# Moving the row ends of one gradient to GpSimd and packing a shift-weight gradient in 32-column tiles

## The chip, the core and the metric

The kernel runs on one core of one Trainium2 chip. Its time is the device time of one execution in microseconds (us); of several executions the median is taken. The engines of the core each work through an instruction queue of their own, in order: TensorE (PE in the profile; its weight loads are PEld), VectorE (DVE), ScalarE (ACT), GpSimd (POOL), and SyncE (SP), which here only issues DMA transfers. The engines wait for each other by semaphores. Matmul results go to PSUM and have to be copied out by DVE or ACT before their PSUM buffer is free again.

## The reference, cut to what matters

The function is a sum of a skip connection, a state-space block with a shift convolution and a long convolution, and a bilinear feed-forward block; the kernel returns its value and nine gradients. With S = 2048 rows, D = 512 channels, F = 1376:

```
xn  = layernorm(x)                                  # x = A_q
ks  = sum_j  shift(k, j) * shift_k[:, j]            # j = 0..3, shift along S
kv  = ks * v
y   = causal long convolution of kv with ssm_k (by FFT), + kv * ssm_D
out = x + xn * y + ((xn Wg) * (xn Wu)) Wd           # out_0
```

From `grad_out` come out_1 (gradient of x), out_2 (k), out_3 (v), out_4 (shift_k, D x 4), out_5 (ssm_k, D x S), out_6 (ssm_D) and out_7 to out_9 (the three weights). Two of them matter here:

- out_1 = grad_out + layernorm backward of dxn. In the kernel each row end is `rstd * dxn + m1`, then `+ grad_out`.
- out_4[d, j] = sum over the sequence of dks[s + j, d] * k[s, d], where dks is the gradient of ks. The kernel takes it from TensorE as the diagonal of small Gram matrices: dks as weights against four shifted copies of k, all products of a group of channels with each other, of which only the diagonal is kept.

## The kernel before, in words

The sequence is laid out as 128 partitions times R = 16 rows. There are three stages. First the inputs are normalised and transformed while the feed-forward block runs chunk by chunk; second the spectral products and their inverse run beside the rest of the feed-forward block. Neither is touched. The third stage, from about 340 us to the end, is the one at hand.

Its backbone is `dw` (L803): for each of 11 blocks of F it transposes the hidden activations (L704, PSUM tile `pt`, copied to `nath` and `natd` by ACT), forms out_9 (L814, `pd`) and out_7 and out_8 (L831, `pu`; the copies are `od` and `og`). The blocks of hidden activations come back from DRAM with `load_hb` (L688). `dw` is a generator of 66 steps, and after each step the side generators of L973 are advanced, each from a first step on and then every so many steps:

- `seq(inv_y(), load_kh(), load_dk())` from step 0, every 3: the inverse transforms `pq` (L729) that give `yC` and, times v, `dks`; then the 2.3 MB load `khC` of k with its three shifted rows (L941 to L943); then two loads `gk` of 1 MB (L769).
- `dsk_gram()` from step 30, every 2: the Gram matrices of out_4. For each of four groups of 128 channels it takes a two-bank PSUM tile `pk` of the pool ps2, and 32 matmuls of 64 columns by 256 (L853): two halves of 64 channels, 16 rows each. DVE multiplies each half by the identity (`kd`, L858) and reduces it (L860).
- `inv_dk()` from step 41, every 3: eight groups of 16 matmuls `po` (L784) for out_5. The even ones are copied to `o5t` by DVE, the odd ones by ACT (L785).
- `ew()` from step 10, every 2: the elementwise ends, from the list `tail`. `final(r)` (L897) first issues the loads of x and of the feed-forward part `bb` for row r + 1 (L892, L894), then forms out_0 (L906 to L909) and dxn with its two row sums (L911 to L919) on DVE. `final2(r)` (L924) applies `rstd` and `m1` on ACT, `final3(r)` (L931) adds grad_out on DVE and stores out_1 from SP (L934). They are run one row late: final2(r - 1), final(r), final3(r - 1). After each two rows `bwd(b)` (L874) computes two rows of out_2: seven DVE operations on `dk` and `tk` and a store (L886).

The PSUM pool ps2 (`P2`) has three buffers, shared by `pt`, `pu`, `pq`, `pk` and `po`; ps1 (`P1`) has two, shared by `pd`, `ptd` and `pts`. A scheduler of the language orders the instructions of each engine from this program; within one engine they then run strictly in that order. So a PE instruction that needs a PSUM buffer waits for the copy that empties it, and that copy waits for everything ahead of it on ACT or DVE. The SBUF pool c2b holds two buffers each of `dxn`, `o1`, `o0`, `bb` and `dk`. `o5t` and `khC` share one buffer (tag o5k). SP's DMAs use eight completion semaphores in turn, so that a DMA is issued only once the eighth one before it has landed.

Of the kernel before, what the change touches and what calls it, by code (L numbers as in the profile page):

```python
# [8 lines left out]
BF = mybir.dt.bfloat16  # L9
F32 = mybir.dt.float32  # L10
I32 = mybir.dt.int32
ALU = mybir.AluOpType
ACTF = mybir.ActivationFunctionType
AX = mybir.AxisListType
# [4 lines left out]
D = 512  # L19
F = 1376  # L20
R = 16
P = 128
NC4 = 4
# [132 lines left out]
def kernel(  # L156
# [24 lines left out]
    nc = tc.nc  # L181
# [10 lines left out]
    o1_n = nat(out_1[0])  # L192
# [9 lines left out]
    def dve(o, i):  # L202
        nc.vector.tensor_copy(o, i)  # L203
# [13 lines left out]
    def P2(name, shape, dt=F32):  # L217
        return ps2.tile(shape, dt, name=name, tag="p2")

    def P1(name, shape, dt=F32):  # L220
        return ps1.tile(shape, dt, name=name, tag="p1")

    ident = const.tile([P, P], BF, name="ident")
# [7 lines left out]
    rstd = const.tile([P, R], F32, name="rstd")  # L231
# [313 lines left out]
    def seq(*its):  # L545
        for it in its:
            for _ in it:
                yield
# [128 lines left out]
    goC = c1.tile([P, R, D], BF, name="goC")  # L677
# [39 lines left out]
    dks = c2.tile([P, R + 3, D], BF, name="dks")  # L717
# [21 lines left out]
    def inv_y():  # L739
        gq = pend  # L740
        todo = [(sg, r0) for r0 in range(0, R, 4) for sg in (0, 1)][2:]
        for r4 in range(0, R, 4):
            gy = gq.pop(0)
            vk = [load_vk(r4), load_vk(r4 + 2)]
            for i in range(0, 4, 2):
                st1p(gy, i, yC[:, r4 + i:r4 + i + 2, :])
            if todo:
                gq.append(load_g1(*todo.pop(0)))
            yield
            gd = gq.pop(0)  # L750
            for i in range(0, 4, 2):
                r0 = r4 + i
                vb, kb = vk.pop(0)
                dd = c2b.tile([P, 2, D], BF, name="dd")
                st1p(gd, i, dd[:])
                nc.vector.tensor_tensor(dks[:, r0:r0 + 2, :], dd[:], vb[:], op=ALU.mult)
                nc.vector.tensor_tensor(kb[:], dd[:], kb[:], op=ALU.mult)
                nc.sync.dma_start(o3_n[:, r0:r0 + 2, :], kb[:])
                if r0 == 2:
                    nc.gpsimd.memset(dks[96:128, R:R + 3, :], 0.0)  # L760
                    nc.sync.dma_start(dks[0:112, R:R + 3, :], dks[1:113, 0:3, :])
                    nc.sync.dma_start(dks[112:127, R:R + 3, :], dks[113:128, 0:3, :])
            if todo:
                gq.append(load_g1(*todo.pop(0)))
            yield
# [8 lines left out]
    def inv_dk():  # L774
        o5t = c2.tile([P, NC4, P, R], BF, name="o5t", tag="o5k")
        o5 = out_5.rearrange("(c q) s -> c q s", q=P)
        steps = [(dh, rh) for dh in range(2) for rh in range(2)]
        for n, (dh, rh) in enumerate(steps):
            gk = gks.pop(0)
            for b in range(2):  # L780
                po = P2("po", [P, 8, P])
                for i in range(8):
                    for c in range(2):
                        nc.tensor.matmul(po[:, i, :], lhsT=gk[:, c, i, cs(b)], rhs=TB.IW[:, c, :], start=(c == 0), stop=(c == 1))  # L784
                (act if b else dve)(o5t[:, 2 * dh + b, :, 8 * rh:8 * rh + 8], po[:].rearrange("q r s -> q s r"))  # L785
                if rh == 1:
                    nc.sync.dma_start(o5[2 * dh + b], o5t[:, 2 * dh + b].rearrange("q s r -> q (s r)"))
                if b == 1 and n + 2 < len(steps):
                    gks.append(load_gk(*steps[n + 2]))
                yield  # L790
            if n == 2:
                yield from put_dD(o5t)
# [52 lines left out]
            yield  # L845

    def dsk_gram():
        for c in range(NC4):
            pk = P2("pk", [P, 2, D])
            for r in range(R):  # L850
                for h in range(2):
                    c0 = c * 128 + 64 * h
                    nc.tensor.matmul(pk[64 * h:64 * h + 64, h, 0:256], lhsT=dks[:, r, c0:c0 + 64],  # L853
                                     rhs=KH[0][:, r:r + 4, c0:c0 + 64], start=(r == 0), stop=(r == R - 1))
            kd = c2.tile([P, 4, 64], F32, name="kd")
            for h in range(2):
                hs = slice(64 * h, 64 * h + 64)
                nc.vector.tensor_tensor(kd[hs], pk[hs, h, 0:256].rearrange("q (j c) -> q j c", j=4),  # L858
                                        ident[hs, hs].unsqueeze(1).to_broadcast((64, 4, 64)), op=ALU.mult)
            nc.vector.tensor_reduce(dsk[:, c, :], kd[:], axis=AX.X, op=ALU.add)  # L860
            yield
        dskb = c2.tile([P, 4, NC4], BF, name="dskb")
        nc.vector.tensor_copy(dskb[:], dsk[:].rearrange("q c i -> q i c"))
        for _ in range(2):
            yield
        pt = P1("pts", [P, 4, P], BF)
        for j in range(4):
            nc.tensor.transpose(pt[:NC4, j, :], dskb[:, 3 - j, :], ident[:])
        dskt = c2.tile([NC4, P, 4], BF, name="dskt")
        dve(dskt[:], pt[:NC4].rearrange("c j q -> c q j"))  # L870
        nc.sync.dma_start(out_4.rearrange("(c p) j -> c p j", p=128), dskt[:])
        yield
# [24 lines left out]
    def final(r):  # L897
        if r + 1 < R:
            load_fin(r + 1)
        o, bb = FL.pop(r)  # L900
        tt = nc.vector.tensor_tensor
        xn = xnC[:, r, :]
        go = goC[:, r, :]
        y = yC[:, r, :]
        m = c2.tile([P, D], BF, name="mf")
        tt(m[:], xn, y, op=ALU.mult)  # L906
        tt(o[:], m[:], o[:], op=ALU.add)
        tt(o[:], o[:], bb[:, 0, :], op=ALU.add)
        nc.sync.dma_start(o0_n[:, r, :], o[:])  # L909
        e = c2.tile([P, D], BF, name="e")  # L910
        tt(e[:], go, y, op=ALU.mult)  # L911
        dxn = c2b.tile([P, D], F32, name="dxn")
        nc.vector.scalar_tensor_tensor(dxn[:], e[:], 1.0, bb[:, 1, :], op0=ALU.mult, op1=ALU.add,
                                       accum_out=s1[:, r:r + 1])
        nc.vector.scalar_tensor_tensor(e[:], dxn[:], 1.0, xn, op0=ALU.mult, op1=ALU.mult,
                                       accum_out=s2[:, r:r + 1])
        nc.vector.tensor_scalar(m2[:, r:r + 1], s2[:, r:r + 1], -1.0 / D, None, op0=ALU.mult)
        nc.vector.tensor_scalar(m1[:, r:r + 1], s1[:, r:r + 1], rstd[:, r:r + 1], -1.0 / D, op0=ALU.mult, op1=ALU.mult)
        nc.vector.scalar_tensor_tensor(dxn[:], xn, m2[:, r:r + 1], dxn[:], op0=ALU.mult, op1=ALU.add)  # L919
        DX[r] = dxn  # L920

    DX = {}

    def final2(r):  # L924
        o1 = c2b.tile([P, D], BF, name="o1")
        nc.scalar.activation(o1[:], DX.pop(r)[:], ACTF.Identity, bias=m1[:, r:r + 1], scale=rstd[:, r:r + 1])
        O1[r] = o1

    O1 = {}

    def final3(r):  # L931
        o1 = O1.pop(r)
        nc.vector.tensor_tensor(o1[:], o1[:], goC[:, r, :], op=ALU.add)
        nc.sync.dma_start(o1_n[:, r, :], o1[:])  # L934

    KH = []

    def load_kh():
        khC = c2.tile([P, R + 3, D], BF, name="khC", tag="o5k")
        nc.gpsimd.memset(khC[0:1, 0:3, :], 0.0)  # L940
        nc.sync.dma_start(khC[:, 3:3 + R, :], k_n)  # L941
        nc.sync.dma_start(khC[1:113, 0:3, :], k_n[0:112, R - 3:R, :])
        nc.sync.dma_start(khC[113:128, 0:3, :], k_n[112:127, R - 3:R, :])  # L943
        KH.append(khC)
        yield

    def every(gen, start, step):
        return [start, step, gen]

    tail = []  # L950
    for b in range(9):
        if b < 8:
            for r in (2 * b, 2 * b + 1):
                tail.append(lambda r=r: (r > 0 and final2(r - 1), final(r), r > 0 and final3(r - 1)))
        else:
            tail.append(lambda: final2(R - 1))
            tail.append(lambda: final3(R - 1))
        if b > 0:
            tail.append(lambda b=b: bwd(b - 1))

    def ew():
        load_fin(0)
        yield
        for f in tail:
            f()
            yield

    def load_dk():
        gks.append(load_gk(0, 0))
        gks.append(load_gk(0, 1))  # L970
        yield

    sides = [every(seq(inv_y(), load_kh(), load_dk()), 0, 3), every(dsk_gram(), 30, 2), every(inv_dk(), 41, 3), every(ew(), 10, 2)]  # L973
    for n, _ in enumerate(dw()):
        for sd in sides:
            if n >= sd[0]:
# [35 lines left out]
```

## Time and profile before

| | us |
|---|---|
| three executions | 529.89, 533.33, 533.99 |
| median | 533.33 |
| the profiled execution | 530.92 |
| its span (first to last instruction) | 528.9 |
| PE busy | 486.2 (92%) |
| DVE busy | 344.9 (65%) |
| ACT busy | 339.2 (64%) |
| POOL busy | 8.5 (2%) |
| third stage, 340 us to the end | 189 |
| PE busy in the third stage | 175.2 |
| DVE busy in the third stage | 119.7 |
| 16 DMA engines, share of the span by SP's queue | 80.3% |

The span is what the profile shows; the execution's own time has 2.0 us around it, and the median lies 2.4 us above that execution. In the profile a group or timeline line gives start, duration, engine, line of the kernel, operation, output and inputs, and in square brackets how long the engine had been idle and who ended it. "Lx" is line x of the kernel before.

### The profile page before, as it was taken

What the parts mean: (1) busy time and instruction counts of PE and PEld (TensorE: products, weight loads), DVE (VectorE), ACT (ScalarE), POOL (GpSimd) and SP (SyncE); (2) the same over time, 40 slices, a digit from 0 to 9 for tenths busy, and PEclk for the clock granted to TensorE, in tenths of its full rate; (3) what the DMA queues carried; (4) which work ended last, traced back from release to release, by engine and by line L of the source; (5) the groups of instructions that cost most, each with busy time, mean ns of one, the idle gap of its engine ahead of it and who ended that gap; (6) DMA issues with size and microseconds to landing.
All of it is one profiled execution on the core that took longest, in us unless ns stands there. A gap on an engine that the chain in (4) does not pass through costs nothing.

```text
span 528.9 us, 10804 instructions
## 1 busy us (share of the span) xinstructions
PE 486.2 (92%) x4409; PEld 322.6 (61%) x4409; DVE 344.9 (65%) x678; ACT 339.2 (64%) x377; POOL 8.5 (2%) x18
## 2 busy tenths in 40 slices
PE   2998999999799999997998999999999999959996
PEld 2876665456436546544535764467677777847885
DVE  5876979876385867837857760042787688899520
ACT  3586798768449859766949861286587444654451
POOL 3100000000000000000000000020000000000000
PEclk9999999999999999998999999999999999989999
DMA  9987988998947967956944459899999998888814
GB/s 284 344 297 290 318 262 315 319 307 311 298 154 260 254 213 257 273 192 217 264 161 147 158 186 405 304 330 325 372 336 311 351 313 268 277 253 252 264 50 133
DMA packets 106570, 140.53 MB, mean 266 GB/s; under 512 B 19001, under 2 KB 79517, under 8 KB 106010
## 3 DMA queue, kind: packets, MB, share of 16 engines
q1 hardware_dynamic: 105194, 139.07, 80.3%
q10 hardware_dynamic: 1328, 0.79, 0.5%
q8 instruction: 34, 0.56, 0.4%
q14 instruction: 14, 0.11, 0.1%
HBM read 72.89 MB, written 63.41 MB: 258 GB/s over the span
## 4 chain that ended last, share of the span: by engine, by line
PE 42%; DMA 22%; DVE 16%; ACT 11%; issue 5%; SPq 3%; DVEq 0%; ACTq 0%
PE px L473 13%; PE pgu L438 7%; PE pu L831 5%; DMA out_dram<-dk 5%; PE py L467 5%; DMA o<-in_A_q_dram 3%; PE pdh L444 3%; ACT SP L200 2%; DMA khC<-in_A_k_dram 2%; DMA out_dram<-o 2%; DMA FD<-fst 2%; PE pd L814 2%; PE pg L531 2%; ACT gu L200 2%; DMA v_b<-in_A_v_dram 2%
## 5 line engine op out<-in xcount | busy, mean ns | idle before, releaser
L831 PE MATMUL pu<-natd,xnC 128*128 128x256 bf16 (+1 forms) x704 | 80.7, 273 | 6.1 <-ACT nath L200 5.9
L473 PE MATMUL px<-WT,hd 128*128 128x512 bf16 (+1 forms) x352 | 81.4, 383 | 0.0
L831 PEld LDWEIGHTS <-xnC 128*128 128x128 bf16 x704 | 68.1, 99 | 15.0 <-issue 6.5
L438 PE MATMUL pgu<-xt,Wu 128*128 128x256 bf16 (+1 forms) x352 | 54.7, 279 | 6.6 <-DVE SP L504 4.1
L473 PEld LDWEIGHTS <-hd 128*128 128x128 bf16 (+1 forms) x352 | 33.8, 98 | 43.5 <-issue 5.2
L200 ACT CAST gu<-pgu 128x1024 bf16<-128x1024 f32 (+1 forms) x48 | 45.4, 946 | 17.3 <-PE pgu L438 16.3
L518 DVE TENSOR_TENSOR T<-SP 128x2048 bf16<-128x2048 bf16 x24 | 29.3, 1222 | 40.2 <-ACT SP L200 40.2
L438 PE MATMUL pgu<-xt,Wg 128*128 128x256 bf16 (+1 forms) x352 | 54.5, 277 | 0.0
L200 ACT COPY natd<-pt 128x2048 bf16<-128x2048 bf16 (+1 forms) x22 | 40.4, 1834 | 19.4 <-PE pt L704 19.4
L200 ACT CAST GO<-pg 128x1024 bf16<-128x1024 f32 x48 | 46.4, 1021 | 4.9 <-PE pg L531 4.6
L444 PE MATMUL pdh<-gt,WdT 128*128 128x256 bf16 (+1 forms) x352 | 48.3, 276 | 1.0 <-DVE WdT L203 0.8
L438 PEld LDWEIGHTS <-Wu 128*128 128x128 bf16 (+1 forms) x352 | 33.9, 102 | 23.5 <-issue 17.8
L200 ACT CAST fst<-pf 128x1024 bf16<-128x1024 f32 x40 | 39.3, 1032 | 8.5 <-DMA FD<-fst 5.2
L200 ACT CAST SP<-ps 128x1024 bf16<-128x1024 f32 x40 | 39.2, 1029 | 4.4 <-PE ps L500 4.3
L467 PE MATMUL py<-Wd,hd 128*128 128x512 bf16 (+1 forms) x176 | 41.8, 379 | 0.0
L814 PE MATMUL pd<-goC,nath 128*128 128x512 bf16 (+1 forms) x176 | 40.1, 379 | 0.0
L444 PEld LDWEIGHTS <-WdT 128*128 128x128 bf16 (+1 forms) x352 | 34.8, 101 | 8.6 <-issue 2.3
L438 PEld LDWEIGHTS <-Wg 128*128 128x128 bf16 (+1 forms) x352 | 35.5, 102 | 4.3
L200 ACT CAST bx<-px 128x512 bf16<-128x512 f32 x16 | 9.5, 593 | 40.9 <-PE px L473 40.9
L453 DVE TENSOR_TENSOR hd<-gu 128x512 bf16<-128x512 bf16 (+1 forms) x48 | 18.9, 396 | 23.7 <-ACT gu L200 23.7
L704 PE MATMUL pt<-ident,hb 128*128 128x128 bf16 (+1 forms) x462 | 30.1, 218 | 1.7 <-ACT yC L200 0.8
L704 PEld LDWEIGHTS <-hb 128*128 128x128 bf16 (+1 forms) x462 | 27.4, 98 | 6.5 <-issue 3.4
(153 smaller groups left out, 692.4 us busy)
## 6 DMA issues: line engine op xcount, KB each, us to landing
HDD<-hd SPq DMA_DIRECT2D x35, 384.0 KB, 3.0
hb<-HDD SPq DMA_DIRECT2D x10, 1344.0 KB, 9.1
FD<-fst SPq DMA_DIRECT2D x24, 512.0 KB, 3.7
X<-FD SPq DMA_DIRECT2D x24, 512.0 KB, 5.2
GD<-GO SPq DMA_DIRECT2D x24, 512.0 KB, 3.7
g<-GD SPq DMA_DIRECT2D x8, 1024.0 KB, 8.9
BX<-bx SPq DMA_DIRECT2D x8, 512.0 KB, 3.6
bb<-BX SPq DMA_DIRECT2D x16, 256.0 KB, 5.4
```

The costliest lines, as they stand in the source:

```text
L200: nc.scalar.copy(o, i)
L438: nc.tensor.matmul(pgu[:w, i, t, :], lhsT=W[:, c, f0:f0 + w], rhs=xt[:, :, c, :], start=(c == 0), stop=(c == NC4 - 1))
L444: nc.tensor.matmul(pdh[:w, i, :], lhsT=WdT[:, c, f0:f0 + w], rhs=gt[:, :, c, :], start=(c == 0), stop=(c == NC4 - 1))
L453: nc.vector.tensor_tensor(hd[:fw, fb0:fb0 + n, 0, :], gu[:fw, :n, 0, :], gu[:fw, :n, 1, :], op=ALU.mult)
L467: nc.tensor.matmul(py[:], lhsT=hd[:fw, fb, 0, ss], rhs=Wd[:fw, fb, :], start=(fb == 0), stop=(fb == NFB - 1))
L473: nc.tensor.matmul(px[:], lhsT=hd[:fw, fb, t, ss], rhs=W[:fw, fb, :], start=(t == 1 and fb == 0), stop=(t == 2 and fb == NFB - 1))
L518: tt(W[:].rearrange("p c a d -> p c (a d)"), A[:, i:i + 1].rearrange("p c a d -> p c (a d)").to_broadcast((P, 2, 2 * D)), B[:].rearrange(" ...
L531: nc.tensor.matmul(pg[q // 2][64 * a:64 * a + 64, q % 2, :], lhsT=TB.EI[32 * q:32 * q + 32, 2 * g + a, yi].rearrange("p k c -> p (k c)"), ...
L704: nc.tensor.transpose(pt[:, r, :fw], hs[:, (r % 2) * 128:(r % 2) * 128 + 128], ident[:fw, :fw])
L814: nc.tensor.matmul(pd[:fw, :], lhsT=nt[:, r, :fw], rhs=goC[:, r, :], start=(r == 0), stop=(r == R - 1))
L831: nc.tensor.matmul(pu[:, c, :, :fw], lhsT=xnC[:, r, cs(c)], rhs=ng[:, :, r, :fw], start=(r == 0), stop=(r == R - 1))
```

## The change

Three edits.

1. The end of each row of out_1 leaves ACT, DVE and SP. GpSimd applies `rstd` and `m1` in place (L924 of the new file), adds grad_out (L925) and issues the store from its own queue (L926). final2 and final3, with their one-row delay, are gone, so that the list `tail` has 24 entries, not 26.
2. The Gram matrices use tiles of 32 weight columns by 128 moving columns: 256 matmuls instead of 128, four of them side by side in four column groups. All sums stand in one PSUM bank, a tile of the pool ps1; DVE multiplies once by a 32-wide diagonal mask and reduces once, instead of eight multiplies and four reductions. The mask is made by four small copies.
3. `load_kh` is a side of its own at step 22 (before, step 24), `load_dk` moves to step 24 (before, 27), and `dsk_gram` starts at step 34 (before, 30).

```diff
     def dsk_gram():
+        diag = c2.tile([P, 32], BF, name="diag")
+        pk = P1("pk", [P, NC4, 4, 32])
+        for h in range(4):
+            hs = slice(32 * h, 32 * h + 32)
+            dve(diag[hs], ident[hs, hs])
         for c in range(NC4):
-            pk = P2("pk", [P, 2, D])
             for r in range(R):
-                for h in range(2):
-                    c0 = c * 128 + 64 * h
-                    nc.tensor.matmul(pk[64 * h:64 * h + 64, h, 0:256], lhsT=dks[:, r, c0:c0 + 64],
-                                     rhs=KH[0][:, r:r + 4, c0:c0 + 64], start=(r == 0), stop=(r == R - 1))
-            kd = c2.tile([P, 4, 64], F32, name="kd")
-            for h in range(2):
-                hs = slice(64 * h, 64 * h + 64)
-                nc.vector.tensor_tensor(kd[hs], pk[hs, h, 0:256].rearrange("q (j c) -> q j c", j=4),
-                                        ident[hs, hs].unsqueeze(1).to_broadcast((64, 4, 64)), op=ALU.mult)
-            nc.vector.tensor_reduce(dsk[:, c, :], kd[:], axis=AX.X, op=ALU.add)
-            yield
+                for h in range(4):
+                    c0 = c * 128 + 32 * h
+                    nc.tensor.matmul(pk[32 * h:32 * h + 32, c], lhsT=dks[:, r, c0:c0 + 32],
+                                     rhs=KH[0][:, r:r + 4, c0:c0 + 32], start=(r == 0), stop=(r == R - 1))
+            if c % 2 == 1:
+                yield
+        kd = c2.tile([P, 4 * NC4, 32], F32, name="kd")
+        nc.vector.tensor_tensor(kd[:], pk[:].rearrange("q c j e -> q (c j) e"),
+                                diag[:].unsqueeze(1).to_broadcast((P, 4 * NC4, 32)), op=ALU.mult)
+        nc.vector.tensor_reduce(dsk[:].rearrange("q c j -> q (c j)"), kd[:], axis=AX.X, op=ALU.add)
...
         nc.vector.scalar_tensor_tensor(dxn[:], xn, m2[:, r:r + 1], dxn[:], op0=ALU.mult, op1=ALU.add)
-        DX[r] = dxn
-
-    DX = {}
-
-    def final2(r):
         o1 = c2b.tile([P, D], BF, name="o1")
-        nc.scalar.activation(o1[:], DX.pop(r)[:], ACTF.Identity, bias=m1[:, r:r + 1], scale=rstd[:, r:r + 1])
-        O1[r] = o1
-
-    O1 = {}
-
-    def final3(r):
-        o1 = O1.pop(r)
-        nc.vector.tensor_tensor(o1[:], o1[:], goC[:, r, :], op=ALU.add)
-        nc.sync.dma_start(o1_n[:, r, :], o1[:])
+        nc.gpsimd.tensor_scalar(dxn[:], dxn[:], rstd[:, r:r + 1], m1[:, r:r + 1], op0=ALU.mult, op1=ALU.add)
+        nc.gpsimd.tensor_tensor(o1[:], dxn[:], go, op=ALU.add)
+        nc.gpsimd.dma_start(o1_n[:, r, :], o1[:])
...
-                tail.append(lambda r=r: (r > 0 and final2(r - 1), final(r), r > 0 and final3(r - 1)))
-        else:
-            tail.append(lambda: final2(R - 1))
-            tail.append(lambda: final3(R - 1))
+                tail.append(lambda r=r: final(r))
...
-    sides = [every(seq(inv_y(), load_kh(), load_dk()), 0, 3), every(dsk_gram(), 30, 2), every(inv_dk(), 41, 3), every(ew(), 10, 2)]
+    sides = [every(seq(inv_y(), load_dk()), 0, 3), every(load_kh(), 22, 1), every(dsk_gram(), 34, 2), every(inv_dk(), 41, 3), every(ew(), 10, 2)]
```

## The prediction

> **What bounds the kernel now.** I read four views. The busy times by stretch come first, since the change lies in the third stage. Columns: stretch, its length, then PE, PEld, DVE, ACT and POOL busy with instruction counts, granted clock, DMA share, GB/s.
>
> ```profile
> 450.00:460.00 10.00, 9.10 (x115) 8.18 (x113) 9.94 (x28) 7.00 (x6) 0.00 (x0) 1.00 0.82 248
> 460.00:470.00 10.00, 9.11 (x100) 6.90 (x98) 8.41 (x22) 3.32 (x4) 0.00 (x0) 1.00 0.73 235
> 470.00:480.00 10.00, 5.45 (x37) 4.20 (x37) 9.34 (x20) 4.82 (x4) 0.00 (x0) 0.66 1.06 342
> 480.00:490.00 10.00, 10.00 (x106) 7.76 (x104) 9.93 (x28) 6.40 (x7) 0.00 (x0) 1.00 0.85 218
> 490.00:500.00 10.00, 9.78 (x115) 8.93 (x113) 4.53 (x8) 5.46 (x4) 0.00 (x0) 1.00 0.99 310
> 500.00:510.00 10.00, 9.81 (x109) 7.40 (x106) 4.86 (x14) 5.70 (x7) 0.00 (x0) 1.00 0.20 68
> ```
>
> PE is full and runs to the end; DMA falls to 0.20 after 500 and DVE has little left. So the end is PE's, and only what delays PE counts. PE has one hole, at 470. PE's timeline shows it (the bracket: idle before, and its releaser), with the Gram matmuls (L853):
>
> ```profile
> 424.11 1.94 PE L853 MATMUL pk<-khC,dks 128*64 128x256 bf16 x32 [1.07 <-DMA khC<-in_A_k_dram]
> 474.55 5.34 PE L831 MATMUL pu<-natd,xnC 128*128 128x256 bf16 x32 [5.44 <-ACT nath L200]
> 480.62 3.66 PE L831 MATMUL pu<-natd,xnC 128*128 128x256 bf16 x32
> 495.01 0.94 PE L704 MATMUL pt<-ident,hb 128*128 128x128 bf16 x14
> ```
>
> `pu` waits for a PSUM buffer that ACT has yet to empty (`nath`). ACT's timeline says why it is late:
>
> ```profile
> 468.35 0.81 ACT L926 ACTIVATE o<-dxn,m,rstd 128x512 bf16<-128x512 f32 x1 [4.27 <-DVE dxn L919]
> 471.45 0.81 ACT L926 ACTIVATE o<-dxn,m,rstd 128x512 bf16<-128x512 f32 x1 [2.28 <-DVE dxn L919]
> 472.17 0.56 ACT L200 CAST od<-pd 128x512 bf16<-128x512 f32 x1
> 472.63 1.86 ACT L200 COPY nath<-pt 128x2048 bf16<-128x2048 bf16 x1
> ```
>
> Two row ends (final2) stand ahead of the copies and wait for DVE's dxn. So DVE's lateness reaches PE through ACT's queue. The second path from DVE to PE is the cast of `po`, which frees the buffer that the `pt` at 495.01 takes:
>
> ```profile
> 491.34 1.23 DVE L203 CAST o5t<-po 128x1024 bf16<-128x1024 f32 x1 [0.27 <-PE po L784]
> 497.70 0.69 DVE L882 TENSOR_TENSOR dk<-dks,skb 128x1024 bf16<-128x1024 bf16 x1 [5.14 <-DMA out_dram<-dk]
> ```
>
> It ended at 492.57, 2.4 us ahead of need. POOL does nearly nothing; its timeline has what I price it by:
>
> ```profile
> 3.55 0.71 POOL L52 IOTA patF<- 128x512 f32 x1
> 15.80 1.79 POOL L268 MEMSET kh<- 1x1536 bf16 x1 [10.99 <-DVE gki L65]
> 345.81 1.37 POOL L940 MEMSET khC<- 1x1536 bf16 x1
> ```
>
> **Part by part.** Sums are made on the profiled execution (span 528.9, own time 530.92); its difference is added to the median, 533.33, which stands 2.4 above that execution.
>
> *The row end leaves ACT.* Sixteen L926 of 0.82 us leave, and the 21.6 us that ACT waited ahead of them. Only the hole counts: 5.44 us, and the 32 `pu` after it took 5.34 instead of 3.66 while the stretch had a clock of 0.66, so 1.7 more: -7.1. Short PE waits for ACT (0.68, 0.22, 0.22) are counted as staying; gone, they give 1.1, the lower end.
>
> *The Gram matmuls.* Before, two matmuls of 256 columns run side by side: 32 in about 1.75 us, 109 ns a pair, 7.0 us for 128. A po block of single 128-column matmuls steps at 56 ns. If four run at once, 64 groups take 3.6 us: -3.4. The `ps` matmuls, 32 weight columns in four column places and two row places, do this: 16 of them took 0.63 us, where 16 one by one at 216 ns would take 3.5. The other end: instructions limited to the present four per 109 ns give 512 x 27 ns = 14, so +7. I take the `ps` row, which is nearest. DVE loses eight kd of 0.42 and four reductions of 0.41 for one of each at twice the columns (0.65 and 0.7) and four mask copies in idle time before 347: about 3.7 us saved, counted with DVE below. That `pk` now holds one of the two ps1 buffers costs nothing: the next `pd` takes the other, and the taker after it is `pts`, which waits for the same sums anyway. Their cast to `dskb` stands by the built order near 444 on DVE; `pts`, at 456.5 before, is due near 452. Without those 8 us PE would wait for it us by us.
>
> *khC at step 22.* The wait of 1.07 goes: in the built order the Gram now stands after the next `pd`, and khC is issued near 405.5, not 411.46. Its three DMAs, and the two gk of 1 MB that now follow before row 6's x, pass row 5's x and the next hidden block on SP's queue. At 342 GB/s (mean of 370 to 430) the 7.9 MB up to row 7's x end at 428.6; that x arrived at 438.7 before. The hidden block is due by 428 against a need at 430. So -1.1, and up to +3 if the block is late.
>
> *Stores on POOL.* Sixteen of about 145 SP issues in this stage go, each 0.34 to 0.47, with SP's waits for L933 behind them. SP is not on PE's path; its relief shows as DVE's earlier loads. On POOL, L924 waits for DVE's L919; behind it stand only the later rows' ends, and two rows on DVE's L913 waits for its dxn buffer. A store is queued behind its own row's two operations, and the next row's waits behind it. POOL has the room: 0.7 + 1.4 + 0.5 = 2.6 per row against a row's pace of 8.
>
> The PE terms sum to -7.1 - 3.4 - 1.1 = -11.6.
>
> *DVE's order.* This takes part of it back. In the built order the third cast of `po` by DVE now stands behind all 16 rows' dxn, where before it stood behind 15 (and behind 50 of the 56 dk and tk operations, as before). PE's `pt`, at 495.01 before, would be due at 483.4, and needs that cast. When does DVE reach it? Row 9's x can be there at 440 (row 7's store, 4.3, and load, 5.1, behind 428.6). From there DVE has 2.2 of row 9, six rows of 3.45 (L906 to L919 by their steps; L933's 0.34 is gone), 24 dk operations of 0.66, and 3.0 of casts: 42, so 482. Waits for dk's two buffers stay: such waits were 9.2 us in all before; I take 5, with stores of 9.0 us: 487. The cast adds 1.2, and from that `pt` to the end of the span lie 33.9 as before: 522.1, so -6.8 in place of -11.6.
>
> *What POOL costs DVE.* No trace row has POOL reading two inputs. POOL's own times I bound by 0.71 for 512 elements written, once for L924 and twice for L925: 2.1 per row. DVE may pay all of it, 9 rows x 2.1 = 19, or nothing. A gain is excluded, since L933 is already counted. The nearest row is the memset of 1.79, which ran beside DVE and took 0.42 more than its twin at 345.81 beside an idle DVE, while the two-input DVE operation in it (L138, 256 elements) took 0.41, no more than the kd of 256 with 0.42. POOL paid there. I take nothing for DVE, and keep 19.
>
> The Trainium skill (SBUF — State Buffer, Who interferes with whom) says that a DVE instruction with two SBUF inputs and a GpSimd instruction that reads SBUF lock each other out for a whole instruction. By that rule DVE pays, and the sum would be the first rival's; the row above had POOL only writing, so it can't refute it.
>
> Sum: 533.33 - 6.8 = 526.5.
>
> **The rivals.**
>
> *POOL's reads hold DVE back (ends slower).* Place: rows 7 to 15. DVE has almost no idle left there (9.94, 9.34, 9.93 of 10), so each us that POOL takes moves the third cast. From 487, 6.8 us more, 0.75 per row, eats the whole gain; at 1.5 per row (13.5) the span is 535.6: 540.0; at 2.1, 545.5. For it: L908, L913, L919 and bwd's operations all read two SBUF tensors. Against: the memset row, and POOL's two operations can fall into dk waits.
>
> *DMA is the limit.* Its share is 1.05 and 0.95 from 370 to 410 and 1.04 to 430; moving khC and gk ahead moves the hidden block and x behind. If the block costs 3 and x of row 9 comes 4 later, 487 becomes 491: 530.5. Against: DMA idles after 500.
>
> *The Gram doesn't run four wide.* Instructions at 27 ns: PE's gain is 1.2 instead of 11.6, and DVE's cast is then in time: 532. At half the speed-up nothing changes, since the cast decides.
>
> **How the numbers follow.** Forecast 0.45, its own range 521.5 (no DVE wait left, small ACT waits gone: -11.8) to 530; POOL holds DVE 0.33; DMA 0.12; Gram 0.10. The range to 541 leaves out the dearest fifth or so of POOL's case and little below: 521 to 541. About 1% (5.3 us) is what a measurement can tell from no change: faster, under 528.0, is nearly all of the forecast, 0.45; within 1% the DMA and Gram cases and under half of POOL's, 0.33; slower the rest, 0.22.
>
> **What would show it.** PE's waits: no 5.44 at L831 behind `nath`, no khC wait; if a `pt` waits for DVE's `o5t`, the size of that wait is the price. Gram matmuls 3 to 4 ns apart in fours, 256 in about 3.6 us. DVE's L908 to L919 longer than 0.42, 0.68 and 0.75 would show POOL's lock; POOL's L924 and L925 over 2.1 together would make it worse. I am wrong if the end is no longer PE's, or if the cast comes after 494.

## The result and the profile after

The changed kernel took 539.15 us (median of six executions, 535.37 to 541.36) against 533.05 for the kernel before (six, 529.89 to 535.32). The ratio on record is 1.0144, with a 95% interval of 1.0106 to 1.0181 (the quotient of the two medians is 1.0114): slower by 1.4%, where 526.5, a gain of 1.3%, had been forecast. The profiled execution has a span of 537.9. Of the runs below, one execution of e8, one of e12 and one of the kernel before beside e9 to e12 fell into a slower state of the chip; the ratios leave them out, the medians don't.

PE's timeline of the changed kernel, third stage, in the lines where it waited or the Gram ran (the Gram is L857 there; its three pieces are 256 matmuls):

```profile
425.40 2.53 PE L857 MATMUL pk<-khC,dks 128*32 128x128 bf16 x168
435.49 1.68 PE L704 MATMUL pt<-ident,hb 128*128 128x128 bf16 x14 [7.55 <-DMA hb<-HDD]
438.69 0.62 PE L857 MATMUL pk<-khC,dks 128*32 128x128 bf16 x29
442.97 1.02 PE L857 MATMUL pk<-khC,dks 128*32 128x128 bf16 x59
470.54 3.65 PE L831 MATMUL pu<-natd,xnC 128*128 128x256 bf16 x32 [0.22 <-ACT nath L200]
481.70 1.65 PE L704 MATMUL pt<-ident,hb 128*128 128x128 bf16 x14 [7.50 <-DVE o5t L203]
502.32 0.95 PE L704 MATMUL pt<-ident,hb 128*128 128x128 bf16 x14 [3.08 <-DVE o5t L203]
```

The hole behind `nath` is gone: what is left of it is 0.22. In its place stand three new holes, 18.1 us together: one for a block of hidden activations that landed late (`hb`), and two for DVE's casts of `po`. In the stretches of the holes or right behind them the granted clock fell to 0.66, 0.70 and 0.83, and the first matmuls behind two of them took 1.68 and 1.65 instead of 0.94 (columns as before: length, PE, PEld, DVE, ACT and POOL busy, clock, DMA share, GB/s):

```profile
430.00:440.00 10.00, 4.44 (x67) 4.20 (x68) 4.92 (x14) 2.53 (x2) 2.50 (x3) 0.66 1.04 340
470.00:480.00 10.00, 3.98 (x38) 3.32 (x36) 9.93 (x18) 2.26 (x2) 5.36 (x6) 0.96 0.86 254
480.00:490.00 10.00, 8.30 (x69) 6.83 (x69) 10.00 (x25) 3.49 (x3) 3.42 (x3) 0.70 0.75 207
500.00:510.00 10.00, 7.68 (x68) 6.13 (x68) 6.29 (x9) 3.25 (x3) 0.59 (x1) 0.83 0.20 73
```

Why the block was late is to be seen in SP's timeline of the changed kernel, where SP issues strictly in order:

```profile
405.93 0.70 SPq L935 DMA_DIRECT2D khC<-in_A_k_dram  x1
411.56 9.21 SPq L769 DMA_DIRECT2D gk<-GD  x2
420.92 4.40 SPq L895 DMA_DIRECT2D o<-in_A_q_dram  x1
426.37 0.39 SPq L688 DMA_DIRECT2D hb<-HDD  x1
```

The two `gk` loads now stand ahead of the block. Issuing them kept SP for 9.21 us (0.61 and 8.50) and the next load for 4.40; the block was issued at 426.37, in the kernel before at 417.74 with `gk` behind it:

```profile
417.74 0.44 SPq L688 DMA_DIRECT2D hb<-HDD  x1
```

Why the second `gk` load took 8.50 stays open. The view of SP's waits puts 6.3 of it down to PE's `pt`, but the last matmuls known to read that buffer, `pq`, had ended at 399.2. In the kernel before the two took 5.47 and the load behind them 3.37, with no wait named.

Why DVE was late is to be seen where its timeline and POOL's are laid side by side. First DVE, with the same operation once alone (422.89) and once beside POOL, then POOL:

```profile
422.89 0.75 DVE L922 SCALAR_TENSOR_TENSOR dxn<-xnC,m,dxn 128x512 f32<-128x512 bf16 x1
445.84 1.64 DVE L922 SCALAR_TENSOR_TENSOR dxn<-xnC,m,dxn 128x512 f32<-128x512 bf16 x1
455.84 1.64 DVE L885 TENSOR_TENSOR dk<-dks,skb 128x1024 bf16<-128x1024 bf16 x1
501.05 1.22 DVE L203 CAST o5t<-po 128x1024 bf16<-128x1024 f32 x1
```

```profile
433.03 0.76 POOL L924 TENSOR_SCALAR dxn<-dxn,rstd,m 128x512 f32<-128x512 f32 x1 [6.39 <-DVE dxn L922]
433.87 1.15 POOL L925 TENSOR_TENSOR o<-dxn,goC 128x512 bf16<-128x512 f32 x1
443.47 2.18 POOL L924 TENSOR_SCALAR dxn<-dxn,rstd,m 128x512 f32<-128x512 f32 x1 [7.57 <-DVE dxn L922]
445.73 1.20 POOL L925 TENSOR_TENSOR o<-dxn,goC 128x512 bf16<-128x512 f32 x1
455.74 1.20 POOL L925 TENSOR_TENSOR o<-dxn,goC 128x512 bf16<-128x512 f32 x1
```

At 433 DVE is idle and POOL takes 0.76 and 1.15. At 443 DVE is dense: POOL's scale drags on for 2.18, and the DVE operation that starts 0.1 us after POOL's add takes 1.64 instead of 0.68 to 0.75. From 340 us on, 21 DVE operations, each with two SBUF inputs, are lengthened so, by 13.5 us together, 11.5 of them after 430. In the kernel before none is (a lengthening counts here from 0.1 us above the usual duration of its line). The last line of DVE's is the third cast of `po`, which the kernel before began at 491.34; the second begins at 480.43, before at 474.99. For these two casts PE waits: the two waits for `o5t` are DVE's lateness.

### The profile page after: what moved, and what is told of

Its sections match the earlier page's. It is cut to its first block, busy times and chain, and to the rows that moved or that the text cites. A ratio compares the mean times of both kernels' runs of the same rounds, so it can differ in the third digit from the quotient of the medians.

```text
span 537.9 us, 11042 instructions
## 1 busy us (share of the span) xinstructions
PE 486.5 (90%) x4537; PEld 323.2 (60%) x4537; DVE 348.3 (65%) x656; ACT 327.6 (61%) x361; POOL 61.6 (11%) x66
## 5 line engine op out<-in xcount | busy, mean ns | idle before, releaser
L831 PE MATMUL pu<-natd,xnC 128*128 128x256 bf16 (+1 forms) x704 | 82.0, 276 | 0.7 <-ACT nath L200 0.7
L473 PE MATMUL px<-WT,hd 128*128 128x512 bf16 (+1 forms) x352 | 80.3, 379 | 0.0
L438 PE MATMUL pgu<-xt,Wg 128*128 128x256 bf16 (+1 forms) x352 | 55.6, 281 | 0.0
L704 PE MATMUL pt<-ident,hb 128*128 128x128 bf16 (+1 forms) x462 | 32.1, 226 | 18.4 <-DVE o5t L203 10.6
L704 PEld LDWEIGHTS <-hb 128*128 128x128 bf16 (+1 forms) x462 | 29.2, 102 | 23.0 <-issue 12.3
L760 POOL MEMSET dks<- 32x1536 bf16 x1 | 1.4, 1372 | 325.3 <-DMA BX<-bx 325.3
```

Of the source, the lines that this page charges most:

```text
L438: nc.tensor.matmul(pgu[:w, i, t, :], lhsT=W[:, c, f0:f0 + w], rhs=xt[:, :, c, :], start=(c == 0), stop=(c == NC4 - 1))
L473: nc.tensor.matmul(px[:], lhsT=hd[:fw, fb, t, ss], rhs=W[:fw, fb, :], start=(t == 1 and fb == 0), stop=(t == 2 and fb == NFB - 1))
L704: nc.tensor.transpose(pt[:, r, :fw], hs[:, (r % 2) * 128:(r % 2) * 128 + 128], ident[:fw, :fw])
L831: nc.tensor.matmul(pu[:, c, :, :fw], lhsT=xnC[:, r, cs(c)], rhs=ng[:, :, r, :fw], start=(r == 0), stop=(r == R - 1))
```

## The experiments

The theory after the result: two prices that the prediction set at nothing. GpSimd's operations lengthen DVE's (price 1, edit 1), and the `gk` loads ahead of the hidden block delay it (price 2, edit 3). Rivals: only one of them counts (A, A'); DVE only waits for its `dxn` buffers or for GpSimd's writes (B); the khC load delays the block by itself. Ratios are against runs of the kernel before on the same chip. Single executions scatter by several us about their median (the profiled ones of e3 and e4 by some 5), so ratios carry the times, and the traces are read for places and durations. The profiled executions also enter the third stage at different moments, which no edit touches: its first `pq` starts at 341.0 in the kernel before, 339.6 in the changed kernel, and between 337.1 (e4) and 343.1 (e3) in the others. So where moments of two runs are compared, they are also counted from that `pq`.

### e1: edit 1 alone

```diff
 kernel before, with final2 and final3 replaced by
+        nc.gpsimd.tensor_scalar(dxn[:], dxn[:], rstd[:, r:r + 1], m1[:, r:r + 1], op0=ALU.mult, op1=ALU.add)
+        nc.gpsimd.tensor_tensor(o1[:], dxn[:], go, op=ALU.add)
+        nc.gpsimd.dma_start(o1_n[:, r, :], o1[:])
```

> The kernel before with edit 1 alone: the row ends on GpSimd; Gram tiles and load steps as before. Theory (two prices: GpSimd's reads lengthen DVE's operations, and the two gk loads ahead of the hidden block delay it): here only the first price is paid. DVE operations reach 1.37 to 1.64 us beside GpSimd's, about 1.4 us per row (12 over rows 7 to 15), and DVE's third cast of po ends near 500 instead of 492.6; the hidden block isn't late. Time 534 to 538. Rival A (only the loads cost): the hole of 5.4 at 470 goes and nothing takes its place, 526 to 528. Rival B (GpSimd's lock costs nothing by itself, DVE only waits for its dxn buffers): DVE operations keep 0.42, 0.68 and 0.75 us, waits ahead of L916 grow instead.

Measured: 532.62 against 531.02, ratio 1.0026 (1.0000 to 1.0053), so a little less than expected. PE's waits in the third stage (line, who was waited for, us in total, times, longest):

```profile
PE po L784 <- DVE o5t L203: 6.4, 2, 4.9
PE pk L853 <- DMA khC<-in_A_k_dram: 2.6, 1, 2.6
```

DVE operations are lengthened by 13.9 us and reach 1.66; the third cast starts at 501.5, in the kernel before at 491.3 (160.6 and 150.3 from the first `pq`). What leaving ACT's queue brought, the casts took back. Rival A falls, and the lengthening speaks against B.

### e2: edits 2 and 3 without 1

> The kernel before with edits 2 and 3: new Gram tiles and new load steps; the row ends stay on ACT, DVE and SP. Theory of two prices: only the second is paid. PE waits 6 to 8 us for the hidden block near 428, the Gram gains 3, no DVE operation is lengthened; time 530 to 536. Rival A' (only GpSimd's lock costs): 522 to 527.

Measured: 531.30, ratio 1.0005 (0.9969 to 1.0042). The time is as expected, the parts only roughly:

```profile
PE pu L831 <- ACT nath L200: 5.1, 3, 3.1
PE pk L857 <- issue: 2.5, 1, 2.5
PE pt L704 <- DMA hb<-HDD: 2.4, 1, 2.4
```

The block cost 2.4 instead of 6 to 8. It wasn't earlier (issued at 428.86, `pt` at 437.06); PE came to it later, after a wait of 2.5 inside the Gram, which has no releaser that the trace shows, and stays open. Without edit 1 PE's holes behind ACT's row ends remain, so the time alone doesn't decide about rival A' here; e3 to e5 do.

### e3, e4, e5: each price taken away, and both

```diff
 e3 and e5, against the changed kernel
-    sides = [every(seq(inv_y(), load_dk()), 0, 3), every(load_kh(), 22, 1), ...
+    sides = [every(inv_y(), 0, 3), every(load_dk(), 27, 1), every(load_kh(), 22, 1), ...
 e4 and e5
-        nc.gpsimd.tensor_scalar(dxn[:], dxn[:], rstd[:, r:r + 1], m1[:, r:r + 1], op0=ALU.mult, op1=ALU.add)
-        nc.gpsimd.tensor_tensor(o1[:], dxn[:], go, op=ALU.add)
+        nc.gpsimd.memset(dxn[:], 0.0)
+        nc.gpsimd.memset(o1[:], 0.0)
```

> The changed kernel with one thing undone: the two gk loads are again issued at step 27, so that they stand behind the hidden block in SP's queue; the shifted k still loads at step 22. Theory of two prices: the wait of 7.5 us at the hidden block shrinks under 2, DVE's loads come some us earlier, but GpSimd's price stays, so that the third cast moves only by what DVE idled for loads between 423 and 438: time 531 to 536. If the khC load itself delays the block, the wait stays at 7 and the time at 537 to 540.

> The changed kernel with GpSimd's two operations per row replaced by two fills with zeros of the same tiles (GpSimd writes but reads nothing; out_1's arithmetic is left out). Order, waits and stores stay. Theory of two prices: DVE operations stay at 0.42, 0.68 and 0.75, the two PE waits for DVE's o5t (7.5 and 3.1) go or fall under 2, the wait for the hidden block stays near 7.5; time 523 to 529. Rival B (the waits for the dxn buffers, or GpSimd's writes, hold DVE): little changes, 535 to 540.

> Both prices taken away together: the changed kernel with the gk loads behind the hidden block and GpSimd's operations replaced by fills with zeros (out_1's arithmetic is left out). Theory of two prices: no PE wait over 2 us is left in the third stage, time 521 to 526, which is what the change would have given without either price. If a third price of 3 us or more exists, the time stays above 528.

Measured ratios:

| | GpSimd's two operations | fills only | difference |
|---|---|---|---|
| gk ahead of the block | 1.0144 (1.0106 to 1.0181), the changed kernel | 0.9997 (0.9972 to 1.0023), e4 | 1.5%, 7.8 us |
| gk behind it | 1.0027 (0.9996 to 1.0057), e3 | 0.9874 (0.9818 to 0.9931), e5 | 1.5%, 8.2 us |
| difference | 1.2%, 6.2 us | 1.2%, 6.6 us | |

(The us are the differences times 533.3.) Each of the four differences is good to 2.4 to 3.4 us by the intervals; as closely as that, the two prices add up: GpSimd's costs 8 us, the late block 6.4, and without both (e5, which leaves out_1's arithmetic out) the change gives 1.3%. Within a row of the table DVE's order is the same. Between the rows it is not: with `gk` behind, 55 of the `dk` and `tk` operations stand ahead of the third cast, not 50. PE's waits of e3, then of e4, then of e5:

```profile
PE pt L704 <- DVE o5t L203: 6.3, 1, 6.3
PE po L784 <- DVE o5t L203: 4.2, 1, 4.2
PE pt L704 <- DMA hb<-HDD: 2.0, 1, 2.0
```

```profile
PE pt L704 <- DMA hb<-HDD: 6.8, 1, 6.8
PE pt L704 <- DVE o5t L203: 2.2, 2, 1.3
```

```profile
PE pt L704 <- DVE o5t L203: 6.0, 1, 6.0
PE pu L831 <- ACT nath L200: 0.7, 3, 0.2
```

Each edit takes away its own wait and leaves the other. With the fills no DVE operation is lengthened, though DVE's order and dependencies are the same, and in the changed kernel itself DVE sits idle ahead of no L916, where it would wait for its `dxn` buffer; so rival B falls. In e3 the block was issued at 415.7, with khC still ahead of it, and waited for no more than 2.0, so the khC load by itself is not the cause (with the stores of out_1 in SP's queue it is another matter, see e8). e4's median of 531.67 lies above its expectation of 523 to 529, and e5 (526.22) missed a part of its own: a wait of 6.0 remains there, for DVE's first cast at 452.73. PE begins its first `po` at 442.8, in the changed kernel at 453.6 (some 9 us earlier, counted from the first `pq`), and DVE hasn't got that far.

DVE's third cast of `po` starts at 501.05 in the changed kernel and 503.09 in e3, but at 489.63 in e4 and 487.13 in e5. Counted from the first `pq` that is 161.5 and 160.0 against 152.5 and 149.5: GpSimd moves it by 9 to 10 us, the place of `gk` by 1.5 to 3.

### e9, e10: which of GpSimd's two operations

e9 keeps only the scale (adding grad_out is left out), e10 only the add (the scale is left out); `gk` stands behind the block.

```diff
 e9
+        nc.gpsimd.tensor_scalar(o1[:], dxn[:], rstd[:, r:r + 1], m1[:, r:r + 1], op0=ALU.mult, op1=ALU.add)
 e10
+        nc.gpsimd.tensor_tensor(o1[:], dxn[:], go, op=ALU.add)
```

> One look at the price of GpSimd's scale: the changed kernel with the gk loads behind the hidden block and only the scale-and-bias (one SBUF tile in, 128x512 f32) left on GpSimd; adding grad_out is left out. If each of GpSimd's instructions shuts DVE out for its own time, DVE's operations are lengthened by up to 0.8 us per row (12 in all); if only an instruction that reads two tiles does, by under 0.45 per row (under 6 in all), with no DVE operation near 1.4 or 1.64.

> One look at the price of GpSimd's add: as the run before, but only the add (two SBUF tiles in, 128x512) left on GpSimd; the scale by rstd and m1 is left out. Theory: one DVE operation per row in the dense stretch is lengthened by 0.96 us and reaches 1.37 or 1.64; 9 to 13 us of lengthening in all, most of the 17.5 that both operations cost.

Measured, one execution each: the scale lengthens ten DVE operations by 3.8 us together, none beyond 1.14; the add lengthens eleven by 9.8, to as much as 1.65. Both as expected: most of the price is the add's, and the scale alone isn't free. (With both, e3 has 15.0 by this count, not the 17.5 of the expectation.) The third cast says the same: counted from the first `pq` it starts at 149.5 with the fills (e5), 153.6 with the scale, 157.6 with the add and 160.0 with both (e3). Each sum is smaller than its operation's time on 16 rows: beside an idle DVE nothing is lengthened, and a meeting costs DVE less than the operation's own time (0.41 of 0.76 for most of the scale's, 0.96 of 1.15 for many of the add's). The sums of the stretch 340 to 540 (length, then PE, PEld, DVE, ACT and POOL busy) of e5, e9 and e10:

```profile
sum 200.00, PE 167.72 PEld 130.44 DVE 110.15 ACT 93.10 POOL 23.35; mean PE 167.72 PEld 130.44 DVE 110.15 ACT 93.10 POOL 23.35
```

```profile
sum 200.00, PE 173.24 PEld 133.96 DVE 113.83 ACT 95.55 POOL 31.66; mean PE 173.24 PEld 133.96 DVE 113.83 ACT 95.55 POOL 31.66
```

```profile
sum 200.00, PE 167.44 PEld 130.19 DVE 119.59 ACT 93.23 POOL 32.86; mean PE 167.44 PEld 130.19 DVE 119.59 ACT 93.23 POOL 32.86
```

The same DVE instructions are busy for 110.15, 113.83 and 119.59 us; in the changed kernel, with both, for 122.51. In e10 a cast that reads PSUM runs beside POOL's add; DVE's line, then POOL's:

```profile
456.17 1.21 DVE L203 CAST o5t<-po 128x1024 bf16<-128x1024 f32 x1
463.79 1.38 DVE L914 TENSOR_TENSOR e<-goC,yC 128x512 bf16<-128x512 bf16 x1
```

```profile
456.00 1.25 POOL L924 TENSOR_TENSOR o<-dxn,goC 128x512 bf16<-128x512 f32 x1 [3.46 <-DVE dxn L922]
463.63 1.26 POOL L924 TENSOR_TENSOR o<-dxn,goC 128x512 bf16<-128x512 f32 x1 [5.52 <-DVE dxn L922]
```

The cast takes its usual 1.21; the product of two SBUF tiles, 0.2 us behind the next add, takes 1.38 instead of 0.42.

### e6, e11: where GpSimd's price reaches PE

```diff
 e6, against e3; e11, against the kernel before
-                (act if b else dve)(o5t[:, 2 * dh + b, :, 8 * rh:8 * rh + 8], po[:].rearrange("q r s -> q s r"))
+                act(o5t[:, 2 * dh + b, :, 8 * rh:8 * rh + 8], po[:].rearrange("q r s -> q s r"))
```

> The changed kernel with the gk loads behind the hidden block and all eight casts of po on ACT; GpSimd's row ends stay as changed. Theory: GpSimd's price of some 12 us of DVE time reaches PE only through DVE's casts of po; with these on ACT, DVE's operations are as long as in the changed kernel, but no pt or po waits for o5t on DVE. Time 521 to 527. Rival: DVE's lateness reaches PE another way (dk buffers, loads behind DVE on SP, ACT's queue), then 530 to 536.

> A control for the version with all casts of po on ACT: the kernel before with that alone. In it no pt waited for DVE's cast, and the hole of 5.4 us was behind ACT's queue, into which four more casts of 1.0 go: time 530 to 535, no gain. If it gains as much as the version with the change (1.4%), the row ends and the Gram have no part in that gain.

Measured: e6 524.26 against 531.60, ratio 0.9863 (0.9797 to 0.9929); e11 531.49 against 531.65, 1.0007 (0.9963 to 1.0052). In e6 DVE is lengthened as ever (16.2 us), and PE waits for none of it:

```profile
PE pt L704 <- ACT og L200: 3.6, 1, 3.6
PE pu L831 <- ACT nath L200: 1.6, 3, 1.2
```

So the casts are the one path by which DVE's lateness reached PE. In the kernel before the same move brings nothing, since its hole (5.1 us in e11) hangs on ACT's row ends.

### e7, e8, e12: other places for the row end

```diff
 e7, against e3 (e12: the same, with e6's casts)
-        nc.gpsimd.tensor_scalar(dxn[:], dxn[:], rstd[:, r:r + 1], m1[:, r:r + 1], op0=ALU.mult, op1=ALU.add)
-        nc.gpsimd.tensor_tensor(o1[:], dxn[:], go, op=ALU.add)
+        nc.vector.tensor_scalar(dxn[:], dxn[:], rstd[:, r:r + 1], m1[:, r:r + 1], op0=ALU.mult, op1=ALU.add)
+        nc.vector.tensor_tensor(o1[:], dxn[:], go, op=ALU.add)
 e8, against e3: final2 and final3 as in the kernel before, on ACT, DVE and SP
```

> The changed kernel with the gk loads behind the hidden block, and the two operations of the row end on DVE in place of GpSimd (store still from GpSimd's queue). DVE has two more operations per row (scale near 0.4 to 0.7, add near 0.7 since one input is f32: together 1.1 to 1.4), which is about what GpSimd's lock costs it (1.4 per row). Theory: time 528 to 534, within 3 us of the version with GpSimd's ends. If the lock costs more than the work itself, it is 5 us faster than that.

> Edits 2 and 3 with the gk loads behind the hidden block; the row ends as in the kernel before (ACT, DVE, SP). No lock, no late block; ACT again has row ends in its queue that wait for DVE. Theory: one or two waits of PE for nath of 2 to 5 us are left, time 523 to 528; the gain against the kernel before is the Gram's 3 us, the wait for khC and what DVE saves.

> A candidate better than both: Gram tiles and shifted k as changed, the gk loads behind the hidden block, the row end's two operations on DVE, its store from GpSimd's queue, all casts of po on ACT. No lock and no PE wait for DVE: PE waits only for ACT (og, nath), 3 to 5 us. Time 519 to 525, the same as or up to 4 us under the version with GpSimd's row ends and casts on ACT, since there DVE's lateness no longer counts.

Measured: e7 527.46 against 531.60, 0.9926 (0.9888 to 0.9965), 5 us under e3. DVE does the row end itself for 19.7 us of busy time more (two operations of 0.54 and 0.69 on 16 rows), and its third cast still starts at 489.85, 13 us earlier than with GpSimd's help (10 counted from the first `pq`). Most of that is DVE's order, which the scheduler built anew: in e7 44 of the `dk` and `tk` operations stand ahead of the third cast, in e3 55, and the last row's end stands behind it. At 0.61 an operation that is some 8 us (an estimate). So e7 doesn't show that the row end is cheaper for DVE on DVE than beside GpSimd: in e3 the lengthening ahead of that cast is 15.0, and 15 rows' ends are some 16 (15 times 1.06, by their steps).

e8 missed its expectation: 534.45, 1.0049 (1.0019 to 1.0079), where 523 to 528 was expected.

```profile
PE pu L831 <- ACT nath L200: 6.2, 2, 5.9
PE pt L704 <- DMA hb<-HDD: 5.9, 2, 3.5
```

With the row ends back on ACT the hole behind `nath` is back, at 5.9; and with their stores back in SP's queue the block was issued at 423.0, not 415.7 as in e3. What held SP between 413.3 and 419.4 is the landing of `khC`, in SP's waits and its timeline:

```profile
SPq L937 <- DMA khC<-in_A_k_dram: 6.1, 1, 6.1
419.44 0.33 SPq L937 DMA_DIRECT2D out_dram<-o  x1
```

That store is the eighth DMA behind khC's first, whose completion semaphore it takes over, and the block stands behind it. In e3 the block is the seventh and goes ahead; the load of x behind it waits 6.1 for khC instead. So beside the stores the khC load does delay the block, and `gk` behind the block brings nothing there (e8 1.0049, e2 1.0005). Taking the row ends off ACT does have a use: edits 2 and 3 bring nothing without it, with `gk` ahead of the block (e2) or behind it (e8).

e12 (four executions) beats both kernels: 519.29 against 531.65, 0.9728 (0.9616 to 0.9839).

```profile
PE pt L704 <- DMA hb<-HDD: 1.4, 2, 0.9
PE pu L831 <- ACT nath L200: 0.7, 3, 0.2
```

No wait of PE in the third stage is over 1 us.

## Why the prediction was wrong

The sum was nearly right for what it priced. The forecast gain was 6.8 us; with both prices taken away (e5) the gain is 1.26%, 6.7 us (interval 3.7 to 9.7). That the two meet so closely is in part luck, as e5's remaining wait is for another cast than the forecast's. Two steps failed.

- **What POOL costs DVE** is the first step that failed: "I take nothing for DVE, and keep 19." It costs 13.5 us of DVE time, 11.5 in the stretch up to the third cast, and 8 us of the kernel's time. The error was the choice of row: a fill reads nothing, and e4 shows that fills indeed cost DVE nothing. The trace showed no case of GpSimd reading, and the value between the bounds of 0 and 2.1 per row was taken from a row of another kind. The price is some 1.3 per row for rows 7 to 15 (11.5 over nine), mostly 0.96 for a DVE operation that meets the add and 0.41 for one that meets the scale. The rule of the Trainium skill that the prediction cited (SBUF — State Buffer, Who interferes with whom), that DVE instructions with two SBUF inputs and GpSimd's reads of SBUF lock each other out, agrees with the trace here: two-input operations are lengthened, 1.38 beside an add against 0.42, a cast from PSUM is not, and fills do nothing.
- **khC at step 22** is the second: "The hidden block is due by 428 against a need at 430. So -1.1, and up to +3 if the block is late." PE needed it at 427.9 and got it at 435.5, a wait of 7.55; by e3 and e5 it costs 6.4 of the kernel's time. The wait for khC did go. The step counted bytes at a rate. But SP's issue of `gk` itself took 9.21 (the cause of which stays open), and the block, behind it in the same queue, wasn't issued before 426.37. e3 shows that the order of `gk` and the block was the cause, not the khC load.
- **The row end leaves ACT** was right: the 5.44 behind `nath` went, to 0.22, in e1 as in the changed kernel; e8 brings it back.
- **The Gram** was right: four run side by side, 168 in 2.53 us (15 ns each); PE's busy time for them falls from 7.8 (four times 1.94) to 4.2, 3.6 against the 3.4 forecast. So the third rival falls.
- **DVE's order** was right in kind: in the changed kernel PE waits for DVE's casts. That the third cast without GpSimd's price starts at 487.13 (e5), where 487 was worked out, is luck: e5's execution enters the third stage 3.4 earlier than the kernel before, and 55 `dk` and `tk` operations stand ahead of the cast in e5, not 50. The step was also incomplete: in e5 PE waits for the first cast, not the third.
- **Stores on POOL** cost nothing that shows: no DVE operation or PE wait hangs on them. What they free is a place in SP's queue (e8).
- **The first rival** gave 540.0 at 1.5 per row, and 539.15 came. That is half a coincidence. Its price per row was near; its effect on the time was too large (8 instead of 13.5: PE's waits for DVE's casts are 10.6 in the changed kernel and 2.2 with the fills), and the late block, which it left out, made up the rest.
- **The second rival** had the block late by 3, for want of DMA rate. It was late by 7.55, and e3 moves the same bytes with a wait of 2.0: the order of issue made it.

## What to carry to other kernels

Work given to GpSimd is not free for DVE: where GpSimd reads SBUF beside a dense DVE, price each such instruction as up to its own length on DVE, and then ask which DVE result PE waits for. Here moving those few casts to ACT made the lengthened DVE harmless. Doing the work on DVE itself cost DVE about as much as GpSimd's help did ahead of the cast that PE waits for (some 16 us, an estimate, against 15.0); that this cast came earlier is for the most part the order of DVE's queue. When a load is moved forward, look at what now stands behind it in its issuing queue and when that is needed, not only at the bytes; where a DMA waits for the landing of the eighth before it, one store more in the queue can decide (e8).

## What the runs showed of the hardware

- GpSimd's scale of 128x512 takes 0.76 beside an idle DVE and its add 1.15. Beside a dense DVE the scale took up to 3.60, over several DVE instructions in a row, not only the one in flight; the add never more than 1.71. DVE pays mostly for the add (9.8 against 3.8 alone), GpSimd mostly for the scale.
- The lengthening hardly depends on the DVE operation: 0.41 to 0.46 in eight of ten cases beside the scale alone (e9), 0.83 to 0.97 in ten of eleven beside the add alone (e10), whether it takes 0.42 or 0.68 when undisturbed.
- GpSimd's fills (0.52) and its DMA issues (0.59) beside DVE lengthened nothing.
- SP's issue of a DMA, mostly 0.3 to 0.6 us, took 9.21 for two loads of 1 MB and 4.40 for the one after, with 2.4 MB of khC just issued ahead of them and the DMA engines full (share 1.03 in 410 to 420); in the kernel before the same took 5.47 and 3.37. Whether the full engines are the cause isn't shown.
